# Three weight turns of a four-pass attention and FFN training step: a 21st buffer for weights, and one more K or V block kept on chip per turn

## The chip, the cores and the metric

The kernel runs on one core of a Trainium2 chip. The metric is device time in microseconds of one execution, and the kernel before has a median of 1938.94 us over three runs (1935.64 to 1939.71). A core has several engines that work side by side: TensorE (PE in the profile, with its weight loads as PEld) multiplies matrices and transposes tiles, VectorE (DVE) and ScalarE (ACT) do elementwise work and move results out of PSUM, GpSimd (POOL) does a little elementwise work and issues the output stores, and SyncE (SP) issues the loads. 16 DMA engines move the data between HBM and the on-chip SBUF.

## The reference

The reference computes two layers forward, and then the gradients of everything. A layer is attention over a long cache followed by a feed-forward block, and both layers use the same weights and the same cache:

```
x = x + attention(layernorm(x), k_cache, v_cache) with wq, wo
x = x + relu(layernorm(x) @ w1 + b1)**2 @ w2 + b2
x = x + attention(layernorm(x), k_cache, v_cache) with wq, wo
x = x + relu(layernorm(x) @ w1 + b1)**2 @ w2 + b2
return x, and its gradients for x, k_cache, v_cache, wq, wo, w1, b1, w2, b2
```

There is one token (x is 1 x 1 x 1024). Attention has 32 query heads in 4 groups of 8; a group shares one key/value head of 65536 positions by 128, in bfloat16. So a K or a V cache of one group is 16 MB, both caches together 128 MB. The hidden width of the feed-forward block is 3584.

## The kernel before

**Four passes and three turns.** The caches don't fit on chip, so they are streamed from HBM four times. Passes 0 and 1 are the forward attention of the two layers (`attn_fwd`, L996), pass 2 is the backward of the second layer's attention with respect to its queries (`attn_bwd3`, L1196), and pass 3 (`attn_bwd4`, L1287) does the rest of the backward work and writes the gradients of both caches. Between the passes lie three turns, in which the weights wq, wo, w1 and w2 are streamed through for the layer norms, the feed-forward blocks and their backward parts. They are opened by `open_dense("dense12")`, `"dense23"` and `"dense34"` (L1637, L1677, L1845), each with a pool of SBUF of its own, and closed by `dst.close()`.

**The arena.** Blocks from the caches and slabs of weights go into one arena of NG = 20 granules of 8 KB per partition, 1 MB each. Granules 0 to 11 (NSLOT) are free for all; 12 to 19 also serve, four per layer, as planes that hold the exponentials of a layer's softmax for a while. A dictionary FREE has, for each granule that is free, the step at which it became so. `take_one` (L292) gives a load the granule that has been free the longest; for output staging (`fill`) it prefers one that came free lately, and in pass 3 it goes by RING, a set of up to NRING = 5 granules that are kept for staging. `take_pair` (L284) gives an aligned pair of granules (2i, 2i+1) whose later half came free first. `kv8` (L351) loads a K or V block where it is first needed in program order: with two neighbouring blocks in one transfer of 2 MB when there is a pair (L366), else alone (L361). The last eight blocks of a pass, and the first 18 of passes 1 and 2, are always loaded alone (`KV["halves"]`, set in `start_pass`, L421). Weights go through `slabs` (L441), whose `fetch` issues the load (L458), and in the second turn through `ch_load` (L1686, load at L1690).

**The order of loads.** SyncE issues all loads in the order in which the program names them. A load waits until the last reader of its granule has finished, and whatever is behind it on SyncE waits with it. TensorE, VectorE and ScalarE keep the written order in passes 0 to 2 and in the second turn; in pass 3 a scheduler may move work.

**Kept blocks.** A pass begins on the side of the cache on which the last one ended. So `plan_keep` (L416) names the first NKEEP[p] blocks of one kind (K, V, V for the three turns) that pass p+1 will need; when pass p has loaded them, `kv_done` doesn't free them. They stay in the arena through the turn. Blocks of the kind that KV["turn"] names are also kept transposed, so that the next pass needs no transposes for them (`turned_to`, L369).

**Reading K and V.** In passes 0 and 1, `kT` transposes a K block on TensorE, eight tiles at a time (L1020), and evacuates them from PSUM into a "kt" tile (pool `ktpool`, four tiles of 2 KB per partition), or in place for a kept block; `kS` multiplies by the queries (L1038), scores go to an S_sb tile, ScalarE takes exponentials (L1103), and `v8` multiplies by V (L1121). In pass 2, V blocks are transposed (L1214) and K blocks multiply (L1268).

**Background.** While a pass runs, weight work for the group before or after is mixed into it: `g_q` and `g_wo` multiply slabs of wq and wo (L515), and `pre_load` issues the first two slabs of the turn's first weight ahead of the pass's end.

**Transposed weights in a turn.** `Rows` (L609) transposes a slab in `front` (L657), evacuates it into a tile "wt" of the turn's pool (L685, NWT = 6 tiles of 2 KB per partition) or in place, and multiplies in `back` (L703, L710). The second turn does w1 in chunks of its own, `ch_turn` (L1704), with eight "wt" tiles (L1711).

The release of a granule, on which the order of loads hangs, is this:

```
def give_slot(i, more=0):
    NOW["step"] += 0.01
    BUSY.discard(i)
    if i not in HELD:
        FREE[i] = NOW["step"] + more
        if PS["pass4"] and NOW["ring"] and len(RING) < NRING:
            RING.add(i)
```

Of the kernel before, what the change touches and what calls it, by code (L numbers as in the profile page):

```python
# [10 lines left out]
BF = mybir.dt.bfloat16  # L11
# [5 lines left out]
P = 128  # L17
# [3 lines left out]
def kernel(  # L21
# [46 lines left out]
    WAIT_STEPS = 5  # L68
    NSLOT = 12
    NWT = 6  # L70
    NKEEP = [8, 7, 7]
    NRING = 5

    const = ctx.enter_context(tc.tile_pool(name="const", bufs=1))
# [2 lines left out]
    ktpool = ctx.enter_context(tc.tile_pool(name="ktpool", bufs=4))  # L77
# [10 lines left out]
    def ps_tr(shape=None, dtype=BF):  # L88
        return PS["pool"].tile(shape or [P, 8, P], dtype, name="ps_tr", tag="tr", bufs=2 if PS["pass4"] else 3)
# [50 lines left out]
    load = {"act": 0.0, "dve": 0.0, "pe": 0.0}  # L140
# [4 lines left out]
    def add_load(act=0.0, dve=0.0, pe=0.0):  # L145
        load["act"] += act
        load["dve"] += dve
        load["pe"] += pe

    def evac(out, in_, kind="bf"):  # L150
        n = 1
        for d in in_.shape[1:]:
            n *= d
        ca = 0.17 + n * 0.00083
        cd = 0.13 + n * (0.00105 if kind == "f32" else 0.00054)

        if PS["pass4"] and kind == "bf":
            ca += 1.5
        if kind == "kta" or kind != "kt" and load["act"] + ca <= load["dve"] + cd:
            load["act"] += 0.17 + n * 0.00083  # L160
            nc.scalar.copy(out=out, in_=in_)  # L161
        else:
            load["dve"] += cd
            nc.vector.tensor_copy(out=out, in_=in_)  # L164


    def col_from_dram(v1d, n, name):
        nj = n // P
        rows = tmp.tile([nj, P], BF, name="rows_c", tag="rows_c")
        nc.sync.dma_start(out=rows[:], in_=v1d.rearrange("(j p) -> j p", p=P))  # L170
        pt = ps_mv([P, nj], BF)
        nc.tensor.transpose(pt[:, :], rows[:, :], ident_b[0:nj, 0:nj])
        col = vec.tile([P, nj], F32, name=name)
        nc.vector.tensor_copy(out=col[:], in_=pt[:])
        return col
# [87 lines left out]
    BLK = J * DH  # L263
    JW = 2 * J
    NG = NSLOT + 2 * G
    assert C * R == BLK
    ARENA = slotp.tile([P, NG * BLK], BF, name="arena")
    GRAN = [ARENA[:, i * BLK:(i + 1) * BLK] for i in range(NG)]
    FREE = {i: 0.0 for i in range(NG)}
    HELD, BUSY, RING = set(), set(), set()  # L270
    NOW = {"step": 0, "pairs": True, "wide": False, "newest": False, "ring": False}
# [18 lines left out]
        return i  # L290

    def take_one(fill, load=False):  # L292
        by_age = sorted((t, i) for i, t in FREE.items())
        if load and NOW["newest"]:
            i = by_age[-1][1]
            del FREE[i]
            return i
        if PS["pass4"]:
            mine = [i for _, i in by_age if (i in RING) == fill]
            i = mine[0] if mine else by_age[0][1] if fill else by_age[-1][1]  # L300
            del FREE[i]
            return i
        if fill:
            ready = [i for t, i in by_age if t <= NOW["step"] - 1]
            i = ready[-1] if ready else by_age[0][1]
        else:
            i = by_age[0][1]
        del FREE[i]
        return i

    def odd_one():
        return any((i ^ 1) not in FREE and t <= NOW["step"] - 16 for i, t in FREE.items())

    class Slot:
        def __init__(self, name, fill=False, at=None, both=False, load=False):
# [100 lines left out]
    def plan_keep(p):  # L416
        if p == 3:
            return set()
        return set([k for k in TOUCH[p + 1] if k[0] == "kvv"[p]][:NKEEP[p]])

# [187 lines left out]
    class Rows:  # L608
# [48 lines left out]
        def front(self, job, kc, slab):  # L657
            L = load
            for q, (k0, w) in enumerate(job["pieces"]):
                pe = w * 0.1  # L660
                if job["vbc"] is not None:
                    n = w * P
                    stt = max(L["dve"] + 0.1 + n * 0.00105, L["act"], L["pe"])
                    tra = max(L["dve"], L["act"] + 0.17 + n * 0.00083, L["pe"] + pe)
                    if stt <= tra:
                        if "y" not in job:
                            self.begin(job)
                        junk = mvs.tile([P, 1024], BF, name="mv_junk", tag="mv_t", bufs=2)
                        nc.vector.scalar_tensor_tensor(out=junk[:, 0:n], in0=slab[:, k0 * P:k0 * P + n], scalar=1.0,
                                                       in1=job["vbc"][:, k0 * P:k0 * P + n], op0=ALU.mult, op1=ALU.mult,  # L670
                                                       accum_out=job["y2"][:, kc, q:q + 1])
                        nc.gpsimd.memset(job["mask"][:, kc, q:q + 1], 0.0)
                        add_load(dve=0.1 + n * 0.00105)
                        self.did(job)
                        continue
                pt = self.ps_wt()
                for i in range(w):
                    nc.tensor.transpose(pt[:, i, :], job["cols"](slab, k0 + i), ident_b[:, :])  # L678
                sl = NOW["slab"]
                if job["inplace"]:  # L680
                    wt = slab[:, k0 * P:(k0 + w) * P].rearrange("p (a b) -> p a b", b=P)
                elif self.views:
                    wt = self.views.popleft()
                else:
                    wt = self.pool.tile([P, 8, P], BF, name="wt", tag="wt", bufs=self.bufs)  # L685
                evac(wt[:, 0:w, :], pt[:, 0:w, :])
                add_load(pe=pe)
                self.queue.append((job, kc, q, wt, sl))
                if job["inplace"]:
                    sl.users += 1  # L690
                else:
                    self.parts += 1
                if self.parts >= self.bufs:
                    yield
# [75 lines left out]
    DENSE = {}  # L770
# [65 lines left out]
    def pipeline(items, stages, bg, end=(), holds=(), lead=None):  # L836

        def due(lag):
            at = {}
            for k, it in enumerate(items):  # L840
                at.setdefault(k + lag + LEAD if lead is None or lag >= 0 else k + ~lag + lead(k), []).append(it)
            return at
        LEAD = 0 if lead is None else lead(len(items))
        when = [due(l) for _, l in stages]
        maxlag = max(l for _, l in stages) + LEAD
        for i in range(len(items) + maxlag):
            NOW["i"] = i
            NOW["wide"] = NOW["pairs"]
            for at, k in holds:
                if i == at:  # L850
                    hold(k)
            tasks(i - 0.5)
            for n, (fn, lag) in enumerate(stages):
                for it in when[n].get(i, ()):
                    fn(*it)
                if n == 0:
                    tasks(i)
            bg.step(max(0, i - LEAD))
            NOW["wide"] = False
            NOW["step"] += 1  # L860
            for before, fn in end:
                if i == len(items) + maxlag - before:
                    fn()
        while TASKS:
            k = min(TASKS)
            NOW["i"] = int(k + 0.5)
            tasks(k)
# [419 lines left out]
    def attn_bwd4(p, La, Lb, on_group, bg, stack, end=()):  # L1287
# [183 lines left out]
        for b in range(V_LEAD * 8 // J // 2):  # L1471
            nexts.append(("k",) + items[(b + 2) * J // 8])
            nexts.append(("v",) + items[(b + NKEEP[2]) * J // 8])
        pipeline(items, [(vT, ~0), (vS, ~TLEAD), (eIn, 0), (eT, TLEAD), (dV8, DV_LAG), (xT, DK_LAG - 1), (dK8, DK_LAG), (k8, B4_LAG)], bg,
# [100 lines left out]
    def open_dense(name):  # L1575
        st = ExitStack()
        DENSE["pool"] = st.enter_context(tc.tile_pool(name=name, bufs=1))
        return st

    x0 = col_from_dram(A_x.rearrange("a b d -> (a b d)"), D, "x0")  # L1580
    b1c = col_from_dram_f(B_b1, F, "b1c")
# [55 lines left out]
    dst = open_dense("dense12")  # L1637
# [21 lines left out]
    L3["n"], L3["nb"], L3["rstd"] = ln_fwd(x2, "L3")  # L1659
    run(g_q(L3, firstg[1], ps_mv))  # L1660
    nc.vector.tensor_copy(out=x3[:], in_=x2[:])
    dst.close()


    reset_load()
# [11 lines left out]
    dst = open_dense("dense23")  # L1677
# [22 lines left out]
    def ch_pe(s):  # L1700

        return DC if s == NCH - 1 else DC - NV

    def ch_turn(s, js=range(4), to=None):  # L1704

        n = ch_pe(s)
        for j in js:
            pt = ps_tr()
            for kc in range(n):
                nc.tensor.transpose(pt[:, kc, :], ch_cols(s, kc, j), ident_b[:, :])  # L1710
            wt = DENSE["pool"].tile([P, 8, P], BF, name="wt", tag="wt", bufs=8)  # L1711
            (nc.vector.tensor_copy if (to[j] if to else j == 3) else nc.scalar.copy)(out=wt[:, 0:n, :], in_=pt[:, 0:n, :])
            w1t[(s, j)] = wt

# [110 lines left out]
    L4["gb"] = vec.tile([P, FC], BF, name="L4_gb")  # L1825
    nc.vector.tensor_copy(out=L4["gb"][:], in_=L4["g"][:])
    nc.vector.tensor_tensor(out=dh4[:], in0=dg4x2[:], in1=L4["r"][:], op=ALU.mult)
    dst.close()


    reset_load()
# [13 lines left out]
    dst = open_dense("dense34")  # L1845
# [31 lines left out]
    rows.add(w1_slabs()[0], DC, FC, lambda: dh2[:], fin_dx1, cols=f_cols, mix=True)  # L1877
    rows.add(wo_slabs(firstg[3])[0], R, DC, lambda: dx1[:], dO_finish(L1, firstg[3]), inplace=True)
    rows.run()
    dst.close()  # L1880
    psA_stack.close()


# [89 lines left out]
```

## Time and profile before

| what | value |
|---|---|
| median of 3 runs | 1938.94 us (1935.64 to 1939.71) |
| the profiled execution, and its span | 1935.05 us, 1933.2 us |
| mean granted TensorE clock | 0.914 |
| busy: PE, PEld, DVE, ACT, POOL | 82%, 67%, 61%, 54%, 7% |
| moved by the DMA engines | 787.63 MB, mean 407 GB/s |
| HBM read, written | 617.62 MB, 165.69 MB |
| pass 0, first turn | to 366 us, to 409 us |
| pass 1, second turn | to 741 us, to 777 us |
| pass 2, third turn | to 1116 us, to 1172 us |
| pass 3 | to 1933 us |

Times in the profile are microseconds from the start of the span. A row of a timeline has its start, its length, the engine, the line of the kernel (L458 is line 458), the operation, what it writes and reads, how many instructions are in the row, and in brackets the idle time before it with what ended it. SPq is SyncE's queue: its rows are the issues of loads, and a long row with several loads is one in which SyncE waited between them. In a row of waits stand the total, the number of times and the longest.

Two rows that the sizes below can be read from, out of the DMA issues (KB each, and median us from issue to landing):

```profile
arena<-in_A_v_cache_dram SPq DMA_DIRECT2D x79, 2048.0 KB, 20.6
out_dram<-arena POOLq DMA_DIRECT2D x149, 1024.0 KB, 16.5
```

### The profile page before, as it was taken

What the parts mean: (1) busy time and instruction counts of PE and PEld (TensorE: products, weight loads), DVE (VectorE), ACT (ScalarE), POOL (GpSimd) and SP (SyncE); (2) the same over time, 40 slices, a digit from 0 to 9 for tenths busy, and PEclk for the clock granted to TensorE, in tenths of its full rate; (3) what the DMA queues carried; (4) which work ended last, traced back from release to release, by engine and by line L of the source; (5) the groups of instructions that cost most, each with busy time, mean ns of one, the idle gap of its engine ahead of it and who ended that gap; (6) DMA issues with size and microseconds to landing.
All of it is one profiled execution on the core that took longest, in us unless ns stands there. A gap on an engine that the chain in (4) does not pass through costs nothing. (4 is left out here: it accounts for less than half of the span.)

```text
span 1933.2 us, 66962 instructions
## 1 busy us (share of the span) xinstructions
PE 1588.5 (82%) x30199; PEld 1304.0 (67%) x30199; DVE 1173.3 (61%) x2451; ACT 1042.0 (54%) x1615; POOL 141.8 (7%) x321
## 2 busy tenths in 40 slices
PE   6878788688778878978787888888987987696977
PEld 6878777688778877877777886555555654454544
DVE  5645555256455554645454577777876886676866
ACT  3434333245333545436363455766876885676765
POOL 0000000000000000000000001111121211121211
PEclk9989999799898989999888999898997998898997
DMA  9999999999999999999999988999999999899998
GB/s 394 427 426 425 429 427 416 398 420 420 428 424 427 427 416 337 391 425 428 426 417 423 407 308 311 425 424 388 424 424 414 420 424 424 341 424 400 425 422 339
DMA packets 107149, 787.63 MB, mean 407 GB/s; under 512 B 9440, under 2 KB 16622, under 8 KB 42222
## 3 DMA queue, kind: packets, MB, share of 16 engines
q1 hardware_dynamic: 82782, 617.65, 77.5%
q0 software_dynamic: 24080, 165.70, 20.5%
q8 instruction: 236, 3.87, 0.7%
q14 instruction: 51, 0.42, 0.1%
HBM read 617.62 MB, written 165.69 MB: 405 GB/s over the span
## 5 line engine op out<-in xcount | busy, mean ns | idle before, releaser
L164 DVE COPY kt<-ps_tr 128x1024 bf16<-128x1024 bf16 x734 | 504.4, 689 | 425.6 <-PE ps_tr L1020 238.2
L161 ACT CAST arena<-ps_gg 128x1024 bf16<-128x1024 f32 x457 | 444.3, 1011 | 184.0 <-PE ps_gg L1424 134.2
L1020 PE MATMUL ps_tr<-ident_b,arena 128*128 128x128 bf16 x3840 | 312.6, 227 | 45.4 <-DMA arena<-in_A_k_cache_dram 30.8
L1020 PEld LDWEIGHTS <-arena 128*128 128x128 bf16 x3840 | 234.9, 101 | 53.6 <-DMA arena<-in_A_k_cache_dram 32.8
L164 DVE CAST arena<-ps_gg 128x1024 bf16<-128x1024 f32 (+2 forms) x186 | 222.3, 1195 | 79.1 <-PE ps_gg L1424 35.5
L161 ACT COPY kt<-ps_tr 128x1024 bf16<-128x1024 bf16 x168 | 176.7, 1056 | 171.1 <-PE ps_tr L1214 108.8
L1424 PE MATMUL ps_gg<-GG,xt 64*128 64x512 bf16 x1024 | 210.6, 409 | 48.0 <-DVE arena L164 32.3
L1121 PE MATMUL ps_acc<-arena 128*128 128x64 bf16 (+4 forms) x4096 | 204.9, 197 | 48.4 <-DMA arena<-in_A_v_cache_dram 33.1
L1038 PE MATMUL ps_sc<-L_qpad,kt 128*128 128x64 bf16 (+7 forms) x3584 | 185.6, 195 | 21.1 <-issue 12.1
L1343 PE MATMUL ps_tr<-ident_b,arena 128*128 128x128 bf16 x1824 | 177.4, 232 | 30.2 <-DMA arena<-in_A_v_cache_dram 27.5
L1103 ACT ACTIVATE arena<-S_sb,L_negm 128x128 bf16<-128x128 f32 x256 | 165.0, 1004 | 63.2 <-DVE L_negm L1088 63.1
L1214 PE MATMUL ps_tr<-ident_b,arena 128*128 128x128 bf16 x2032 | 163.6, 226 | 40.0 <-DMA arena<-in_A_v_cache_dram 37.0
L1121 PEld LDWEIGHTS <-arena 128*128 128x128 bf16 x4096 | 160.1, 101 | 53.8 <-DMA arena<-in_A_v_cache_dram 37.5
L1343 PEld LDWEIGHTS <-arena 128*128 128x128 bf16 x1824 | 116.8, 103 | 87.6 <-issue 55.6
L1038 PEld LDWEIGHTS <-kt 128*128 128x128 bf16 x3584 | 154.6, 101 | 25.7 <-issue 14.3
L1214 PEld LDWEIGHTS <-arena 128*128 128x128 bf16 x2032 | 123.6, 101 | 45.4 <-DMA arena<-in_A_v_cache_dram 39.6
L1455 PEld LDWEIGHTS <-arena 128*128 128x128 bf16 x2048 | 92.2, 101 | 56.3 <-issue 38.5
L1424 PEld LDWEIGHTS <-xt 64*128 64x128 bf16 x1024 | 64.8, 94 | 95.4 <-issue 57.5
L1103 ACT ACTIVATION_READ_ACCUMULATOR arena<-S_sb,L_negm 128x1 f32 x256 | 127.8, 499 | 0.0
L583 ACT ACTIVATE mv_t<-mv_t 128x1024 bf16<-128x1024 bf16 x96 | 102.1, 1065 | 38.8 <-DVE mv_t L594 38.7
L1268 PE MATMUL ps_acc<-dsT,arena 128*128 128x64 bf16 (+7 forms) x2048 | 102.8, 194 | 11.4 <-DMA arena<-in_A_k_cache_dram 7.1
L1380 PE MATMUL ps_sc<-DOB,kt 128*128 128x64 bf16 (+3 forms) x1824 | 112.0, 197 | 0.1
(318 smaller groups left out, 2127.6 us busy)
## 6 DMA issues: line engine op xcount, KB each, us to landing
arena<-in_A_k_cache_dram SPq DMA_DIRECT2D x82, 2048.0 KB, 21.0
arena<-in_A_v_cache_dram SPq DMA_DIRECT2D x79, 2048.0 KB, 20.6
out_dram<-arena POOLq DMA_DIRECT2D x149, 1024.0 KB, 16.5
arena<-in_A_v_cache_dram SPq DMA_DIRECT2D x84, 1024.0 KB, 13.5
arena<-in_A_k_cache_dram SPq DMA_DIRECT2D x84, 1024.0 KB, 14.5
arena<-in_A_wo_dram SPq DMA_DIRECT2D x22, 1024.0 KB, 15.4
arena<-in_B_w_dram SPq DMA_DIRECT2D x21, 1024.0 KB, 10.1
arena<-in_A_wq_dram SPq DMA_DIRECT2D x18, 1024.0 KB, 13.9
```

The lines of the kernel that those rows point to most:

```text
L161: nc.scalar.copy(out=out, in_=in_)
L164: nc.vector.tensor_copy(out=out, in_=in_)
L583: nc.scalar.activation(out=t[:, :], in_=t[:, :], func=ACTF.Copy, accum_out=y[:, kc:kc + 1])
L1020: nc.tensor.transpose(pt[:, i, :], kb8[:, i, :], ident_b[:, :])
L1038: nc.tensor.matmul(state["ps_s"][:, s:s + w, :].rearrange("p a b -> p (a b)"), lhsT=kt[:, i, :], rhs=L["qpad"][:, g, 0:w, :].rearrange("p ...
L1103: nc.scalar.activation(out=E(p, g, c0, SU)[:, :, h], in_=S[:, h, :], func=ACTF.Exp, bias=L["negm"][:, g, su, h:h + 1], scale=SCALE, accum_ ...
L1121: nc.tensor.matmul(ps_o[:, 0:w, :], lhsT=vb8[:, i, :], rhs=E(p, g, c, w), start=(c % SU == 0), stop=(c % SU == SU - 1), skip_group_check=True)
L1214: nc.tensor.transpose(pt[:, i, :], vb8[:, i, :], ident_b[:, :])
L1268: nc.tensor.matmul(ps_dq[:, 0:w, :].rearrange("p a b -> p (a b)"), lhsT=kb8[:, i, :], rhs=dsT[:, s:s + w, :].rearrange("p a b -> p (a b)") ...
L1343: nc.tensor.transpose(pt[:, i, :], vb8[:, i, :], ident_b[:, :])
L1380: nc.tensor.matmul(state["ps_dp"][:, s:s + w, :].rearrange("p a b -> p (a b)"), lhsT=vt[:, i, :], rhs=DOB[:, g, 0:w, :].rearrange("p a b - ...
L1424: nc.tensor.matmul(pg[:, 512 * h:512 * h + 512], lhsT=xt[64 * h:64 * h + 64, j1 // 8 + m, :], rhs=gg[64 * h:64 * h + 64, :, :].rearrange(" ...
```

## The change

In each turn the pool of the turn gets one tile more, `turn_gran` of 8 KB per partition. `open_dense` appends it to the granules as number NG (20) and puts it into FREE with time 0.0, so that it is the granule that has been free the longest; `close_dense` takes it out again. Only weights can take it: `take_one` leaves it out for loads of K and V blocks and for output staging, and `odd_one` doesn't count it. The room comes from the transposed tiles: the function `wt_tile` hands out, in turn, one of the four kt tiles, which lie idle in a turn, and one of four wt tiles of the turn's pool, where six or eight wt tiles were before. And NKEEP goes from 8, 7, 7 to 9, 8, 8: in each turn one more block (K in the first, V in the other two) stays in the arena, in which the weights now leave one granule less.

```diff
-    NKEEP = [8, 7, 7]
+    NKEEP = [9, 8, 8]
...
     def take_one(fill, load=False):
-        by_age = sorted((t, i) for i, t in FREE.items())
+        by_age = sorted((t, i) for i, t in FREE.items() if i < NG or not (fill or load))
...
     def odd_one():
-        return any((i ^ 1) not in FREE and t <= NOW["step"] - 16 for i, t in FREE.items())
+        return any((i ^ 1) not in FREE and t <= NOW["step"] - 16 for i, t in FREE.items() if i < NG)
...
-                    wt = self.pool.tile([P, 8, P], BF, name="wt", tag="wt", bufs=self.bufs)
+                    wt = wt_tile()
...
     def open_dense(name):
         st = ExitStack()
         DENSE["pool"] = st.enter_context(tc.tile_pool(name=name, bufs=1))
+        GRAN.append(DENSE["pool"].tile([P, BLK], BF, name="turn_gran"))
+        FREE[NG] = 0.0
+        DENSE["n"] = 0
         return st
+
+    def close_dense(st):
+        del FREE[NG]
+        GRAN.pop()
+        st.close()
+
+    def wt_tile():
+        DENSE["n"] += 1
+        if DENSE["n"] % 2:
+            return ktpool.tile([P, 8, P], BF, name="kt", tag="kt")
+        return DENSE["pool"].tile([P, 8, P], BF, name="wt", tag="wt", bufs=4)
...
-    dst.close()
+    close_dense(dst)
...
-            wt = DENSE["pool"].tile([P, 8, P], BF, name="wt", tag="wt", bufs=8)
+            wt = wt_tile()
```

`dst.close()` becomes `close_dense(dst)` at the end of all three turns.

More of the change, by code (lines that the diff above doesn't have):

```diff
@@ L1827 @@
     nc.vector.tensor_tensor(out=dh4[:], in0=dg4x2[:], in1=L4["r"][:], op=ALU.mult)
-    dst.close()
+    close_dense(dst)
     reset_load()
@@ L1879 @@
     rows.run()
-    dst.close()
+    close_dense(dst)
     psA_stack.close()
```

## The prediction

> **What bounds the kernel now.** The page's slices come first: the row of the DMA engines reads 9 nearly throughout, the last row 420 to 429 GB/s inside the passes.
>
> ```profile
> PE   6878788688778878978787888888987987696977
> DMA  9999999999999999999999988999999999899998
> GB/s 394 427 426 425 429 427 416 398 420 420 428 424 427 427 416 337 391 425 428 426 417 423 407 308 311 425 424 388 424 424 414 420 424 424 341 424 400 425 422 339
> ```
>
> The reader is to see that TensorE has idle tenths and the DMA engines hardly any. At 428 GB/s a block of 1 MB (1,048,576 bytes) takes 2.45 us, so a block that is not loaded can be worth at most 2.45 us, and only where TensorE waits for loads later on. The dips, slices 16, 24, 25 and 35, are the places where it may be worth nothing. (The Trainium skill, "DMA: Bandwidth & Descriptors", section "Where 436 GB/s comes from", says that loads from HBM are bound at about 358 GB/s per core; this trace moves 428, so the measurement decides. By the page a block would be worth 2.93 us and the sum below 0.5 us lower.)
>
> Then the waits of TensorE at the end of the first pass, and SyncE's own queue there:
>
> ```profile
> PE ps_acc L1121 <- DMA arena<-in_A_v_cache_dram: 10.0, 4, 6.4
> ```
>
> ```profile
> 304.71 0.33 SPq L366 DMA_DIRECT2D arena<-in_A_v_cache_dram  x1
> 318.41 0.33 SPq L366 DMA_DIRECT2D arena<-in_A_k_cache_dram  x1
> 326.85 0.33 SPq L366 DMA_DIRECT2D arena<-in_A_v_cache_dram  x1
> 327.23 17.62 SPq L361 DMA_DIRECT2D arena<-in_A_v_cache_dram  x6
> 347.44 3.28 SPq L458 DMA_DIRECT2D arena<-in_A_wo_dram  x2
> 351.72 1.27 SPq L361 DMA_DIRECT2D arena<-in_A_v_cache_dram  x2
> 353.46 14.52 SPq L458 DMA_DIRECT2D arena<-in_B_w_dram  x5
> 336.59 0.34 PE L515 MATMUL ps_bg<-run_ob,arena 128*128 128x1 bf16 x8
> ```
>
> The first shows 10.0 us of waiting for V blocks between 326 and 366 us, 6.4 of them at once: this tail is bound by loads. The second shows how they are issued. SyncE issues in program order, and each load waits for its granules; L366 rows are pairs (2 MB), L361 rows single blocks. The last row is the last read of a weight block of the background, which matters below. At the third turn the chain is different:
>
> ```profile
> 1114.87 1.06 PE L1268 MATMUL ps_acc<-dsT,arena 128*128 128x64 bf16 x32 [1.18 <-DMA arena<-in_A_k_cache_dram]
> 1108.24 46.55 SPq L458 DMA_DIRECT2D arena<-in_B_w_dram  x15
> 1116.38 0.17 DVE L1192 SCALAR_TENSOR_TENSOR L_dqT<-dqa,L_rZ 128x8 f32<-128x8 f32 x1
> 1117.74 0.31 PEld L1868 LDWEIGHTS <-arena 128*128 128x128 bf16 x8
> ```
>
> The pass ends on its last K block, the first weight slab of the turn has been issued 8 us earlier, and L1868 reads it 1.2 us after the pass's last VectorE read (L1192).
>
> **The change part by part.**
>
> *Bytes.* Three blocks fewer are loaded: at most 3 × 2.45 = 7.4 us. Each place decides what of it shows.
>
> *Tail of the first pass.* Kept blocks leave the arena's free list. Eight K blocks are four whole pairs; the ninth is the lower half of a fifth pair, in granules 6 and 7. Keeping 6 strands 7, and every later pair load has to take the next pair that comes free. Following the allocator's rule (the pair whose later half came free first) by hand, the pair loads of before at 287.53, 298.99, 304.71 and 318.41 move about one release later, to 299, 304.7, 318.4 and 326.8. They hide: the queue of transfers is deep (the page has 20.6 us from issue to landing for a V pair). The last pair load, V6/7, issued at 326.85, now finds only granules 8 and 9, and the later of them is held by the background weights until L515 at 336.59 + 0.34 = 336.93. V8, V9 and V10, behind it on SyncE, wait too though their own granules are free. The DMA engines have then finished what was issued before: V8 landed at 342.17, and two transfers of 2.45 and 4.9 us (V8, V6/7) before that is 334.8. So they run dry for some 2 us, and a pair load into idle engines takes longer than its share: 437.12 to 446.69 = 9.6 us and 814.99 to 824.43 = 9.4 us, two rows of this trace. V6/7 lands at 336.9 + 9.5 = 346.4 instead of about 339.7. Behind it come V8 to V11, four blocks: 346.4 + 4 × 2.45 = 356.2, where V11 landed at 351.06: +5.1 us. TensorE reads V11 until 353.5, so by then it has caught up with the loads and nothing covers the delay; the blocks behind stay back to back, and the wait of 6.4 us for V14 (landed at 363.43) moves to 368.5. Ends: 0, if another pair is free by 327 or the queue hides it; and +7.8, if the pair's later half comes free with the V block released at 339.68, 2.7 us after. I take +5.1, the value for the release that the rule gives. (The Trainium skill, same page, "Anatomy of one DMA — SWDGE (gpsimd) path", gives a DMA as 2.0 us plus bytes over 436 GB/s, 6.8 us for a pair, though for GpSimd's queue; SyncE's rows here have 9.4 to 9.6. By the page this term would be 2.7 us smaller.)
>
> *First turn and second pass.* The first w1 slab goes to the new granule. It lies where the score tiles S_sb lay, and their last read, the exponentials of L1103, ends at 353.9; before, the slab was issued at 353.46: 0.5 us in a queue of 10 us or more, nothing. After the turn one K load is gone, and the four transposes and evacuations that its turned columns would need. TensorE is the bound until 487 us (no wait for a load from 386 to 487), and loads after it, up to waits at 735 to 743; what the DMA engines don't move is saved there: −2.45 us. The other end is 0, if the lead is lost at a dry spot such as 437 us (0.4 us long).
>
> *Second turn and third pass.* The first w1 chunk waits for L1103 at 731.3 instead of going out at 725.87. The following issues reach 734.8 anyway and land behind wo at 743, so I cost it at nothing; if that queue were empty it would cost 5.4. After the turn V7 is not loaded, and K1 to K3 go out one release later (769.7, 772, 776.4 become 772, 776.4, 777.5). From 743 to 844 us TensorE never waits for a load, and at 815 the DMA engines are idle already because V9's granule comes late:
>
> ```profile
> 815.00:817.50 2.50, 1.81 (x48) 1.69 (x45) 2.06 (x5) 2.50 (x6) 0.00 (x0) 1.00 0.77 210
> ```
>
> The last two columns are the DMA share and GB/s. That release is a TensorE transpose, which the saved block does not bring forward, so the saved 2.45 us lengthens this idle time. I take 0; ends −2.45 and 0.
>
> *Third turn.* V8 stays, so the tail's seven loads before the weights move one release later each (up to 5.7 us against 7 to 10 us of queue): hidden, 0. But the first w2 slab now takes the new granule, which lies over tiles of attn_bwd3; the last read is L1192, until 1116.55. Issued then instead of at 1108.24, into engines that have 313 GB/s of work, it lands 4.94 us later (one lone block: 768.14 to 773.08) at 1121.5 instead of 1117.33; the slab behind it at about 1124 instead of 1121.09. L1868 and the transposes at 1117.7 are late by 3.8 us; the back half of the wq work (L710 and the layer norm after it) can run in that time. Ends 0 and +3.8; I take +2.4, nearer the upper, since TensorE is busy 2.50 of 2.50 us from 1117.5 and its order is fixed.
>
> *Fourth pass.* One more V block is on chip: −2.45 if loads bind. But the arena's granules serve the staging of gradients too: two granules are free at the pass's start, one goes to the Xs slot, and until the first group ends the ring of staging buffers (five) is effectively four. Stores take 16.5 us from issue to landing, and the pass already waits for them:
>
> ```profile
> ACT arena L161 <- DMA out_dram<-arena: 12.7, 4, 4.7
> DVE arena L164 <- DMA out_dram<-arena: 4.4, 1, 4.4
> ```
>
> Those 17.1 us with five buffers lie between 1205 and 1395; with four, each wait grows by up to a fifth of the turnaround, 3.3 us. Some of it hides behind other work of two engines. Ends −2.5 and +6; I take +0.5, near the row of loads (few of TensorE's waits here name a load) but with one wait of 3 us showing.
>
> *Transposed tiles.* Alternating four old kt tiles with four own ones gives eight in turns two (eight before) and one and three (six before); kt tiles idle in a turn. Same evacuations, same instructions: 0, ends −0.5 and +0.7 (one wait of kind "ps_bg L710 <- ACT wt", 0.7 the longest).
>
> **Sum.** +5.1 − 2.45 + 0 + 2.4 + 0.5 = +5.5 us on the profiled execution (1935.05 us; span 1933.2, 1.85 around it), that is 1940.6. The median of the three runs, 1938.94, lies 3.9 above that execution, and runs of the same kernel spread by as much; I set the sum on the median: 1944.4 us. Sum of the low ends: −8; of the high ends: +18.
>
> **The rivals.**
>
> *The bytes show, the tails hide* (the other side). If another pair of granules is free at 327 us, or the queue still holds 5 us of transfers when V6/7 waits, the +5.1 falls. Speaks for it: the page's 20 us from issue to landing, and 0.99 to 1.0 DMA share up to 345. Against: transfers issued by 326.85 end at 334.8 by the landing times. It decides when V6/7 is issued before about 330. Then −2.45 at the first turn, −2.45 at the fourth pass, up to −2.45 at the second turn, +0 to 2 at the third: about −6, 1933.
>
> *All cancels.* The tail costs half (V6/7 lands in 7 us as the queue is not quite dry), the third turn nothing: +2.5 − 2.45 = 0, 1939. For: three of four places have something behind which to hide.
>
> *The ring of four binds.* With 149 output stores of 1 MB, if the early waits grow by 3.3 us on each of the five times shown, little hidden: +10 for that part, +15 in all, 1954. Against: the pass's order is free, the shortage ends with the first group.
>
> **How the numbers follow.** A change under 0.2% (3.9 us) is about what a measurement of this kernel can't tell from none. Forecast (+3.9 to +10) 0.47, ring 0.10: slower 0.57. Bytes show (−3.9 or less) 0.25: faster. Cancel 0.18: same. The range for 8 in 10 reaches from the bytes' case, 1933, to between forecast and ring, 1954; the forecast's own range is 1942.8 to 1949.
>
> **What would show it.** After: SyncE's issue of V6/7 at about 337 and a window at 335 to 338 with a DMA share well below 0.9; pass one's last wait of TensorE for V14 ending near 368; a first w2 slab issued after the last read of attn_bwd3 and a wait of L1868 of some 3 us; HBM reads lower by 3.1 MB (617.62 before); the stretch from the first turn's end to 735 shorter by about 2.5; an idle DMA at 815 some 2 us longer. The prediction is wrong if V6/7 goes out by 330, if the turn-three slab finds its room free before 1112, or if the fourth pass gains its 2.45.

## The result

The changed kernel takes 1980.56 us (median of five runs, 1977.13 to 1984.06), the kernel before 1938.94 us in the runs beside it: a ratio of 1.022, 95% interval 1.0208 to 1.0233, some 42 us slower. The profiled execution of the changed kernel took 1982.43 us with a span of 1980.7, so the two profiled executions are 47.4 us apart. Times from the traces below are set against that.

The page of the changed kernel, first the header, the engines and the slices, then what HBM moved:

```profile
span 1980.7 us, 66833 instructions
...
PE 1605.6 (81%) x30135; PEld 1307.8 (66%) x30135; DVE 1174.3 (59%) x2445; ACT 1040.5 (53%) x1613; POOL 142.0 (7%) x321
...
DMA  9999999999999999999999978898999999999997
GB/s 394 426 428 426 428 427 374 381 413 424 427 425 428 427 402 318 371 426 427 424 427 422 353 278 324 311 395 344 408 424 416 415 425 424 347 424 375 424 421 290
...
HBM read 614.48 MB, written 165.69 MB: 394 GB/s over the span
```

The reads fell from 617.62 to 614.48 MB, three blocks, as they should. The time did not follow: the same rate as in the slices of before stands in most places, and the new dips are slices 7 (the end of pass 0, 374 where there were 416), 23 and 24 (the third turn, 353 and 278 where there were 407 and 308), and 26 and 28 (the start of pass 3, 311 and 344 where there were 425 and 388). A slice is 49.5 us here.

Where the 47.4 us arise can be read by following the same piece of work through both traces: the end of the last V product of passes 0 and 1 (L1121), of the last K product of pass 2 (L1268), and the issues of the first, eighth and last big output stores of pass 3.

| work | before, us | after, us | late by | added here |
|---|---|---|---|---|
| last V product of pass 0 | 367.7 | 372.7 | 5.0 | 5.0 |
| last V product of pass 1 | 738.9 | 743.0 | 4.1 | −0.9 |
| last K product of pass 2 | 1115.9 | 1125.3 | 9.3 | 5.2 |
| first store of pass 3 | 1184.1 | 1199.1 | 15.0 | 5.7 |
| eighth store | 1214.3 | 1253.9 | 39.6 | 24.6 |
| last store | 1926.9 | 1974.3 | 47.4 | 7.8 |

So half of the loss arises between the first and the eighth store of pass 3, which are 30 us apart before and 55 after.

**The tail of pass 0.** SyncE's issues in the changed kernel, and the share of the DMA engines, first in the kernel before and then in the changed one (last columns: granted clock, DMA share, GB/s):

```profile
326.87 0.33 SPq L366 DMA_DIRECT2D arena<-in_A_k_cache_dram  x1
327.25 0.43 SPq L361 DMA_DIRECT2D arena<-in_A_v_cache_dram  x1
336.81 0.33 SPq L366 DMA_DIRECT2D arena<-in_A_v_cache_dram  x1
337.19 18.02 SPq L361 DMA_DIRECT2D arena<-in_A_v_cache_dram  x5
```

```profile
335.00:337.50 2.50, 2.50 (x75) 2.50 (x75) 1.48 (x5) 0.18 (x2) 0.00 (x0) 1.00 1.04 433
```

```profile
335.00:337.50 2.50, 2.50 (x80) 2.50 (x78) 1.48 (x5) 0.33 (x2) 0.00 (x0) 1.00 0.54 220
342.50:345.00 2.50, 0.00 (x0) 0.00 (x0) 0.00 (x0) 0.27 (x2) 0.00 (x0) 0.76 0.95 393
```

The pair of V6 and V7 (the third row) goes out at 336.81 and landed at 346.51, the DMA engines are half idle at 335 to 337.5, and TensorE does nothing at all from 342.5 to 345. The single block of the second row is V8, which the program names after that pair: SyncE's order is not strictly that of the program, contrary to what the text ahead of the prediction says.

**The third turn.** SyncE and TensorE's longest wait:

```profile
1123.08 2.55 SPq L458 DMA_DIRECT2D arena<-in_B_w_dram  x2
1125.90 0.33 SPq L458 DMA_DIRECT2D turn_gran<-in_B_w_dram  x1
1127.35 1.32 SPq L458 DMA_DIRECT2D arena<-in_B_w_dram  x2
1139.41 0.33 SPq L458 DMA_DIRECT2D turn_gran<-in_B_w_dram  x1
```

```profile
PE ps_acc L1882 <- DMA turn_gran<-in_B_w_dram: 3.7, 1, 3.7
```

The slab in the new granule is issued at 1125.90, when the pass has ended, and landed at 1134.09; L1882 is the line that was L1868. It is the first slab of w2 that the program names, since the new granule counts as free the longest, but two slabs named after it (first row) had gone out ahead of it. SyncE then stands still from 1128.67 to 1139.41, until the new granule has been read and can be loaded again.

**The start of pass 3.** The waits for output stores between 1180 and 1320 us, first in the kernel before, then in the changed one:

```profile
ACT arena L161 <- DMA out_dram<-arena: 9.6, 4, 4.0
DVE arena L164 <- DMA out_dram<-arena: 6.7, 2, 4.4
```

```profile
ACT arena L161 <- DMA out_dram<-arena: 26.3, 5, 9.7
DVE arena L164 <- DMA out_dram<-arena: 2.7, 1, 2.7
```

The first two stores in the kernel before:

```profile
1184.10 0.58 POOL L1430 DMA_DIRECT2D out_dram<-arena  x1 [6.43 <-DMA arena<-in_A_k_cache_dram]
1190.26 0.53 POOL L1430 DMA_DIRECT2D out_dram<-arena  x1 [1.50 <-ACT arena L161]
```

And in the changed kernel, with the first wait between them:

```profile
1199.07 0.58 POOL L1430 DMA_DIRECT2D out_dram<-arena  x1 [6.43 <-PE ps_tr L1358]
1206.51 1.93 ACT L161 CAST arena<-ps_gg 128x1024 bf16<-128x1024 f32 x2 [9.75 <-DMA out_dram<-arena]
1214.71 0.53 POOL L1430 DMA_DIRECT2D out_dram<-arena  x1 [10.29 <-ACT arena L161]
```

The first store, issued at 1199.07, landed at 1206.41; 0.1 us later ScalarE, which stood for 9.75 us, goes on. The trace calls every granule "arena"; by the allocator's rules, followed in program order, it is the same granule that is filled again. The second store is 15.6 us behind the first, where before it was 6.2 us.

### The profile page after: what moved, and what is told of

Its sections match the earlier page's. It is cut to its first block, busy times and chain, and to the rows that moved or that the text cites. A ratio compares the mean times of both kernels' runs of the same rounds, so it can differ in the third digit from the quotient of the medians.

```text
span 1980.7 us, 66833 instructions
## 1 busy us (share of the span) xinstructions
PE 1605.6 (81%) x30135; PEld 1307.8 (66%) x30135; DVE 1174.3 (59%) x2445; ACT 1040.5 (53%) x1613; POOL 142.0 (7%) x321
## 3 DMA queue, kind: packets, MB, share of 16 engines
q0 software_dynamic: 24080, 165.70, 20.1%
HBM read 614.48 MB, written 165.69 MB: 394 GB/s over the span
## 5 line engine op out<-in xcount | busy, mean ns | idle before, releaser
L164 DVE COPY kt<-ps_tr 128x1024 bf16<-128x1024 bf16 x724 | 497.5, 689 | 445.0 <-PE ps_tr L1020 237.9
L161 ACT COPY kt<-ps_tr 128x1024 bf16<-128x1024 bf16 x178 | 185.7, 1048 | 198.7 <-PE ps_tr L1214 110.3
L164 DVE CAST arena<-ps_gg 128x1024 bf16<-128x1024 f32 (+2 forms) x190 | 226.6, 1193 | 82.4 <-PE ps_gg L1424 43.5
L1121 PE MATMUL ps_acc<-arena 128*128 128x64 bf16 (+4 forms) x4096 | 202.5, 195 | 55.7 <-DMA arena<-in_A_v_cache_dram 33.8
L1424 PE MATMUL ps_gg<-GG,xt 64*128 64x512 bf16 x1024 | 217.0, 427 | 30.2 <-ACT arena L161 15.1
L1343 PE MATMUL ps_tr<-ident_b,arena 128*128 128x128 bf16 x1792 | 181.1, 236 | 38.0 <-DMA arena<-in_A_v_cache_dram 24.8
L1214 PE MATMUL ps_tr<-ident_b,arena 128*128 128x128 bf16 x2032 | 165.9, 228 | 41.6 <-DMA arena<-in_A_v_cache_dram 37.8
L1121 PEld LDWEIGHTS <-arena 128*128 128x128 bf16 x4096 | 157.8, 100 | 58.9 <-DMA arena<-in_A_v_cache_dram 37.2
L1038 PE MATMUL ps_sc<-L_qpad,kt 128*128 128x64 bf16 x3520 | 178.8, 193 | 18.7 <-issue 11.6
L1038 PEld LDWEIGHTS <-kt 128*128 128x128 bf16 x3520 | 148.7, 100 | 24.1 <-issue 14.6
L1380 PEld LDWEIGHTS <-kt 128*128 128x128 bf16 x1792 | 84.7, 103 | 50.5 <-issue 50.0
L1455 PE MATMUL ps_acc<-X,arena 128*128 128x64 bf16 (+3 forms) x1536 | 98.5, 198 | 21.2 <-DMA arena<-in_A_k_cache_dram 21.2
```

Of the source, the lines that this page charges most:

```text
L1038: nc.tensor.matmul(state["ps_s"][:, s:s + w, :].rearrange("p a b -> p (a b)"), lhsT=kt[:, i, :], rhs=L["qpad"][:, g, 0:w, :].rearrange("p ...
L1121: nc.tensor.matmul(ps_o[:, 0:w, :], lhsT=vb8[:, i, :], rhs=E(p, g, c, w), start=(c % SU == 0), stop=(c % SU == SU - 1), skip_group_check=True)
L1214: nc.tensor.transpose(pt[:, i, :], vb8[:, i, :], ident_b[:, :])
L1343: nc.tensor.transpose(pt[:, i, :], vb8[:, i, :], ident_b[:, :])
L1380: nc.tensor.matmul(state["ps_dp"][:, s:s + w, :].rearrange("p a b -> p (a b)"), lhsT=vt[:, i, :], rhs=DOB[:, g, 0:w, :].rearrange("p a b - ...
L1424: nc.tensor.matmul(pg[:, 512 * h:512 * h + 512], lhsT=xt[64 * h:64 * h + 64, j1 // 8 + m, :], rhs=gg[64 * h:64 * h + 64, :, :].rearrange(" ...
```

## The experiments

Delays at "the first store" and the like are set against the profiled execution of the kernel before, as above. Kernels that run the same program up to some point differ there from one profiled execution to the next: halves and both below, which are the same up to pass 3, are 4.2 and 9.2 us late at the end of pass 2, and 1.7 and 9.3 at a quarter of it. So a difference of 5 us in one trace says little; ratios are over the runs.

**k877: the buffer and the shared tiles, no block more.**

```diff
-    NKEEP = [9, 8, 8]
+    NKEEP = [8, 7, 7]
```

> The 21st buffer and the shared transposed tiles stay, but as many K and V blocks are kept as before (8, 7, 7). Theory (the blocks kept cost the tail of pass 0 and the start of pass 3; the buffer costs a wait for the pass's end at each turn): nothing at the tail of pass 0 (the last V product of the pass at 366 us as before), some +3, +4 and +3 to +6 us at the three turns, nothing at the start of pass 3; about +8 to +12 us in all. Rival (the buffer is free, all is the kept blocks): within 2 us of before. Rival (alternating the transposed tiles costs): as the first in total, but the time comes inside the turns, not at the first slab.

Measured: 1946.53 us against 1937.91, ratio 1.005 (1.0035 to 1.0066). The end of pass 0 is as before (0.0), the first and second pass end within 0.3; then +4.1 at the end of pass 2, +8.1 at the first store, +6.2 at the eighth. So without the kept blocks the tail of pass 0 and the start of pass 3 lose nothing, and the buffer by itself costs some 8.6 us, from the second turn on. The +3 expected at the first turn are not there.

**k878: only the third turn keeps one more.**

```diff
-    NKEEP = [9, 8, 8]
+    NKEEP = [8, 7, 8]
```

> As the change, but only the third turn keeps one more block (8, 7, 8). Theory: the tail of pass 0 as before; about +30 us between the end of pass 2 and the end of the first group of pass 3; +34 to +40 us in all. Rival (the losses need the earlier delays, each pass entering late): +20 us or less.

Measured: 1978.51 us, ratio 1.0203 (1.0179 to 1.0227), 40 us slower. First store +10.4, eighth +36.6: the step of 26 us in the first stores is there in full though the first store is only 10 us late. Against k877 the one V block kept costs 32 us.

**late: the new buffer is handed out last.**

```diff
-        FREE[NG] = 0.0
+        FREE[NG] = NOW["step"] + 0.04
```

> The change (9, 8, 8), but the new buffer is handed out after the granules that are free when the turn opens, not first. Theory (the first slab waits in the new buffer for the pass's last instruction, and SyncE's queue behind it): the three turns lose 3, 4 and 3 to 6 us less, so about +30 to +33 us instead of +42; the tail of pass 0 keeps its +5. Rival (the turns lose because a granule is missing, whatever the order): still +40 to +44 us.

Measured: 1972.76 us, ratio 1.0181 (1.0157 to 1.0204): +35 us, 7 us better than the change, between the +30 to +33 of the theory and the +40 to +44 of the rival. By place: between the end of pass 2 and the first store 1.1 us instead of 5.7, between the end of pass 1 and that of pass 2 1.9 instead of 5.2, as expected; but pass 1 ends 9.9 us late instead of 4.1, which was not expected and is not explained. The tail keeps its +5.3.

**less: one early load of pass 3 is left to its due time.**

```diff
             nexts.append(("v",) + items[(b + NKEEP[2]) * J // 8])
+        nexts.pop()
```

> The change (9, 8, 8), but of the four early loads that pass 3 issues into freed granules the last V block is left to its due time, so its granule goes to the staging of outputs. Theory (the first group of pass 3 has one staging granule until others come free, and its stores follow one another): 15 to 25 us of the 42 go away, +17 to +27 us left. Rival (pass 3 is late because its first K loads are issued 16 us late): no better than +38 us.

Measured: 1961.93 us, ratio 1.0128 (1.0107 to 1.0149), +24 us: 17.6 better than the change. The first store is as late as there (+14.9), the fourth is 12.5 late instead of 27.8, the eighth 20.0 instead of 39.6. So entering the pass 15 us late isn't what costs 24.6 us; one granule for staging at the start takes most of it away, and 5.1 us are left between the first and the eighth store. Its stores (to be held against the two of the changed kernel above):

```profile
1198.99 0.58 POOL L1430 DMA_DIRECT2D out_dram<-arena  x1 [6.43 <-PE ps_tr L1358]
1205.15 0.53 POOL L1430 DMA_DIRECT2D out_dram<-arena  x1 [1.49 <-ACT arena L161]
```

**starved: the kernel before, with a granule less for staging.** Three granules are free after pass 3's first K loads, one of which the Xs slot takes; of the two that are left for staging one is withheld until the group ends.

```diff
         RING.update(sorted(FREE)[:2])
+        away = sorted(FREE)[1]
+        del FREE[away]
...
                 state["Xs"].free()
+                give_slot(away)
```

> The kernel before (8, 7, 7, no buffer, own transposed tiles), but one of the two free granules that pass 3 begins with is withheld until its first group ends. Theory (staging starved of granules is what costs 25 us at the start of pass 3): 15 to 25 us slower than before, all of it between the first and the sixteenth store, and nothing at all before 1190 us. Rival (that loss comes from entering pass 3 late, by 15 us, with its loads): within 4 us of before.

Measured: 1976.35 us against 1938.03, ratio 1.0199 (1.0179 to 1.022): 38 us slower, more than the 15 to 25 expected. The first store is 2.3 late, the fourth 20.1, the sixteenth 24.8: the step expected, at the place expected. After that it goes on to 37.2 at the thirty-second and 45.0 at the fortieth store, which was not expected, and then stays there (46.5 at the sixty-fourth, 43.6 at the 128th). So it grows only while the granule is away: in program order the first group ends some forty stores in. The waits of ScalarE and VectorE for stores between 1180 and 1320 us:

```profile
ACT arena L161 <- DMA out_dram<-arena: 31.2, 5, 10.4
DVE arena L164 <- DMA out_dram<-arena: 3.5, 1, 3.5
```

They are close to those of the changed kernel (26.3 and 2.7), in a kernel that has neither the buffer, nor the tiles, nor a block more. One granule fewer for staging brings about a loss nearly as large as that of the whole change, though its second half, after the sixteenth store, has no counterpart there.

**bless: the other direction.** The kernel before with the same edit as in "less": a third granule for staging.

```diff
             nexts.append(("v",) + items[(b + NKEEP[2]) * J // 8])
+        nexts.pop()
```

> The kernel before, but of the four early loads of pass 3 the last V block is left to its due time, so staging has three granules at the start of the first group instead of two. Theory (staging binds there): the waits of ScalarE and VectorE for stores, 17 us between 1205 and 1395, shrink by some us, and the total is 0 to 6 us faster than before; a third granule is worth less than the second, which was worth 20 to 45. Rival (loads bind there): the V block that comes later costs 2.5 us or more.

Measured: 1938.25 us against 1938.00, ratio 1.0006 (0.9993 to 1.0019): no difference. The waits for stores between 1180 and 1320 go from 9.6 and 6.7 to 8.0 and 5.4 us. The second granule is worth about 40 us (starved), the third, at the start of the group, nothing that can be measured. The ring's limit of five is the same in both.

**halves: V6 and V7 of pass 0 loaded alone.**

```diff
-        KV["halves"] = set(TOUCH[p][-8:] + (TOUCH[p][:18] if p else []))
+        KV["halves"] = set(TOUCH[p][-10 if p == 0 else -8:] + (TOUCH[p][:18] if p else []))
```

> The change (9, 8, 8), but in pass 0 the blocks V6 and V7 are loaded alone, not as a pair. Theory (the ninth kept block strands half a pair, and the pair load of V6 and V7 waits for granules 8 and 9, with SyncE's queue behind it): V6 is issued at about 327 us instead of 337, the pass's last V product comes at 368 us as before the change instead of 373, and the total is 3 to 6 us better than the change. Rival (the tail is late because a granule is missing): the last V product stays at 372 to 373 us.

Measured: 1972.52 us, ratio 1.0177 (1.0163 to 1.0191), +34.5 us: 7 better than the change, a little more than the 3 to 6 expected. SyncE and the DMA engines:

```profile
326.49 0.33 SPq L366 DMA_DIRECT2D arena<-in_A_k_cache_dram  x1
326.87 20.70 SPq L361 DMA_DIRECT2D arena<-in_A_v_cache_dram  x8
```

```profile
335.00:337.50 2.50, 2.50 (x80) 2.50 (x77) 1.48 (x5) 0.38 (x2) 0.00 (x0) 1.00 1.02 423
```

V6 goes out at 326.87, the share at 335 to 337.5 is 1.02 instead of 0.54, and the last V product comes at 367.7, +0.0. With as many kept blocks and as many granules the loss is gone: it was the pair's wait.

**tiles: the shared transposed tiles alone.** The kernel before with `wt_tile` in both places and no new granule.

```diff
-        GRAN.append(DENSE["pool"].tile([P, BLK], BF, name="turn_gran"))
-        FREE[NG] = 0.0
...
-        del FREE[NG]
-        GRAN.pop()
```

(against the changed kernel, with NKEEP = [8, 7, 7])

> The kernel before (8, 7, 7) with the shared transposed tiles alone: alternately one of four kt tiles and one of four wt tiles, no 21st buffer. Theory (the tiles cost nothing; what the kernel with the buffer and 8, 7, 7 lost, +8.6 us, is the buffer's waits): within 2 us of before. Rival (the alternation costs): +4 to +9 us.

Measured: 1938.09 us against 1938.03, ratio 1.0001 (0.999 to 1.0012). The tiles cost nothing.

**k877late: the buffer handed out last, no block more.** The edits of k877 and late together.

> 8, 7, 7 kept blocks with the buffer, handed out after the granules that are free when a turn opens. Theory (the first slab waits in the buffer for the pass's last ScalarE instruction): the second turn loses 0 to 2 us instead of 4, the third 0 to 2 instead of 4, and the total is within 5 us of before (the kernel with the buffer first was 8.6 us slower). Rival (having the buffer in the rotation costs, wherever it stands): +7 to +10 us as before.

Measured: 1941.56 us against 1938.00, ratio 1.0015 (1.0002 to 1.0028): about 3 us slower, where the buffer handed out first was 8.6. From the end of pass 2 to the first store nothing is added (k877: 4.0), as expected. But at the end of pass 2 its trace is 5.5 late (k877: 4.1), so the second turn is not better; what the buffer costs there is not settled.

**both: the two repairs together.** The edits of halves and less.

> The change (9, 8, 8) with V6 and V7 of pass 0 loaded alone and the last of the four early V blocks of pass 3 left to its due time. Theory (two separate losses): the gains of the two edits add, +42 less 8 less 18 = about +14 to +20 us. Rival (one hides the other): +22 us or more.

Measured: 1958.08 us, ratio 1.0107 (1.0085 to 1.0129), +20 us. Against the change's +41.6 that is 21.5 us better, where the two alone give 7.1 and 17.6: they add up but for 3 us, at the upper end of the theory's range. In its trace, 24.9 us longer than that of the kernel before, 13.7 arise ahead of the first store, 4.8 between the first and the eighth, the rest later.

**only1: the change in the first turn alone**, with the repair of the tail: 9, 7 and 7 blocks, the buffer and the shared tiles in the first turn, the old tiles in the others, V6 and V7 loaded alone.

```diff
-        GRAN.append(DENSE["pool"].tile([P, BLK], BF, name="turn_gran"))
-        FREE[NG] = 0.0
+        if name == "dense12":
+            GRAN.append(DENSE["pool"].tile([P, BLK], BF, name="turn_gran"))
+            FREE[NG] = 0.0
```

> The buffer and the shared tiles in the first turn alone, 9 K blocks kept there, 7 and 7 V blocks with the old tiles in the others, and V6 and V7 of pass 0 loaded alone. Theory: no loss at the tail of pass 0 (0 +- 1 us), at most +1 us at the first turn, and 2.45 us of loads fewer in pass 1: 0 to 3 us faster than before. Rival (a block that is not loaded is worth nothing even where loads bind): 0 to 3 us slower.

Measured: 1940.30 us against 1938.03, ratio 1.0014 (1.0003 to 1.0024): about 2 us slower, on the rival's side. In its trace pass 0 ends 1.9 late and pass 1 0.3 early. That would be 2.2 us gained, near the 2.45 of the block, but within what one trace differs from the next, so the gain is not shown, nor where the time goes. No version with the buffer beat the kernel before.

## Why the prediction was wrong

It forecast slower, which held, but by 5.5 us (range 1933 to 1954), where 42 were measured. The direction held mainly for another reason than the one forecast: the sum came to "slower" through the tail of the first pass, and most of the loss lies in a term that was put at +0.5. By its steps:

- **Tail of the first pass, +5.1: right in place and cause, and in size only at its end.** V6/7 was issued at 336.81 (forecast 336.9), landed at 346.51 (346.4), V14 landed at 368.45 (368.5), the last V product is 5.0 late. halves shows the cause. The way from the one to the other was not the one worked out. V8 had gone out ahead of the pair, at 327.25, so three blocks stood behind it instead of four, and V11 landed at 353.79, not at 356.2: 2.7 late. The rest came because V12 and V13, which by the allocator's rules take the granules of V6 and V7, went out at 351.62 and 354.88 instead of 339.69 and 344.52; the blocks behind did not stay back to back. The rule from the Trainium skill, "DMA: Bandwidth & Descriptors", "Anatomy of one DMA — SWDGE (gpsimd) path", would have had this pair land after 6.8 us; it took 9.7, issued by SyncE. But it was not alone, and nor were the two pairs from which the 9.5 us were taken: the next loads were issued 0.4 us behind it here, 0.5 and 3.1 us behind there, so a pair by itself was not measured. (The side remark that a block of 2.93 us makes the sum 0.5 us lower leaves out the four blocks that are added in this term; with them the sum would be 1.4 us higher.)
- **First turn and second pass, −2.45: not seen.** −0.9 in the trace of the change, and between +0.8 and +1.8 in halves, less and both, which keep nine K blocks and hand the buffer out first too; +0.3 in k877 without the block; only1 alone has −2.2. The forecast that the buffer's first slab waits for the last exponentials (353.9) was wrong: it was issued at 373.25, beside the last instructions of the pass on VectorE and ScalarE (L1161 and L1166, 373.0 to 373.5), and SyncE stood still for it from 363.5. That this cost little is k877's +0.3. Here and in the second turn the room of the closed pool came free with the pass, not with the last reader of the one tile beneath.
- **Second turn and third pass, 0: mis-sized.** 5.2 us in the change. The first chunk of w1 went out at 743.60, not at 731.3, for the same reason. Kernels without the buffer in this turn add 0.5 to 2.3 at this place (tiles, only1, starved, bless), those that hand it out first 3.4 to 7.6 (halves, k877, less, the change, both, k878), with means 3.7 us apart. That the buffer costs some us here is shown; that its wait is the reason is only argued, since handing it out last did not help in k877late.
- **Third turn, +2.4: right in mechanism, 5.7 in this trace.** L1882 waits 3.7 us for the slab in the new granule, near the upper end of 3.8. The five other kernels that hand the buffer out first add 2.5 to 4.5 here, those without it −0.7 to 1.8, and handing it out last takes the loss to 1.1 (late) and 0.0 (k877late).
- **Transposed tiles, 0: right** (tiles, 1.0001).
- **Fourth pass, +0.5 with ends −2.5 and +6: this is the step that failed; it measured 32 us**, 24.6 of them within eight stores. The mechanism was named, "the ring of staging buffers (five) is effectively four", and also stood as a rival with 10 us. What was wrong is the number of buffers at the start. The ring is five granules only later; the first group begins with as many as are free just then, two in the kernel before. The prediction wrote "two granules are free at the pass's start, one goes to the Xs slot" and still reckoned with a fifth of a turnaround, where the step is from two to one. With one, there is nothing to fill while its store is under way, and the first stores follow the landing of the one before: ScalarE goes on at 1206.51 and 1220.09, 0.1 us after the first and the second store landed (1206.41 and 1219.99). The runs close this: starved (one granule less in the kernel before, +38 us), less (one more in the changed kernel, −17.6), k878 (the third turn's block alone, +40).
- **The sum's ends, −8 to +18.** They failed through the same term, which had 6 as its upper end and measured 32. The 17 us of waits for stores were read as a price that grows by a share. But their sum is no price: between 1180 and 1320 us it is 16.3 us in the kernel before, 25.6 in less and 29.0 in the change, which add 0, 5.1 and 24.6 us in the first eight stores.

By the allocator's rules, followed in program order, all thirteen kernels sort themselves. Between the first and the eighth store the five that begin with one staging granule (the change, k878, late, halves, starved) add 21.9 to 26.2 us, the four others that begin with two (k877, k877late, tiles, only1) −1.9 to 1.5, and bless with three −1.3. less and both begin with two as well, but one granule of the ring stays with the Xs slot until the first group ends, so that from the fourth fill on they have what the prediction reckoned with, a ring of four: they add 5.1 and 4.8. So what it priced was about as large as its upper end of 6, and what it left out, the start, is the rest, nearly 20 us. (less and both also load one V block later, so the 5 us are not the ring's alone.)

Open: why the loss of starved grows from 25 to 45 us between the sixteenth and the fortieth store, while that of the changed kernel, which lacks a granule just as long, stays (39.6 at the eighth, 38.5 at the fortieth); what the buffer costs in the second turn; and pass 1 of late.

## What to carry to other kernels

A buffer taken away is priced by how many are free at that moment, not by the nominal size of the pool: count them by hand at the first use, because from two to one a pipeline becomes a chain of fill and store, while from three to two it may cost nothing. When blocks are kept across a stage, check both ends: what the allocator can pair in the stage that gives them up, and what the stage that inherits them finds free. A transfer saved is not yet time saved: no version here that loads less was faster than the kernel before. And a new buffer has a wait of its own, for whatever lay in its room; while it lasts, the loads behind it on the same queue stand still.

## What the hardware showed that was not expected

TensorE's busy time rose, from 1588.5 to 1605.6 us, with 64 matmuls fewer, and the mean granted clock fell from 0.914 to 0.900. Two windows of the changed kernel in the first group of pass 3 (the last three columns: granted clock, DMA share, GB/s):

```profile
1235.00:1275.00 40.00, 33.19 (x262) 18.37 (x260) 27.61 (x40) 27.04 (x35) 5.53 (x10) 0.62 0.77 296
1275.00:1315.00 40.00, 35.71 (x383) 21.08 (x383) 25.72 (x49) 25.52 (x29) 6.60 (x13) 0.74 0.98 378
```

Over 1180 to 1340 us the clock is 0.73 in the changed kernel and 0.74 in starved, 0.83 in less, and 0.87 before. In the same stretch one and the same matmul, that of L1424, takes 505 ns in the mean in the changed kernel and 426 before. So this stage, where it stalls for stores, also computed more slowly, and the loss is more than the added waits: 12.7 us of them between 1180 and 1320 (29.0 against 16.3), beside 24.6 us of delay in the first eight stores alone. The Trainium skill, "TensorE: Matmul & The Clock Gate", section "What's actually happening", has the array at half rate by default and after an idle window of about 3.4 us. Mean clocks of 0.62 and 0.73 agree with a mixture of half and full rate, but no run here separates the clock's part from that of the waits.
